# Two 64-row chunks side by side in every transposed tile of a fused attention and FFN kernel

## The chip, the cores and the metric

The kernel runs on one core of a Trainium2 chip. The metric is the device time of one execution in microseconds (us). Shown are the median of three runs and one profiled execution, with the trace of every engine: PE (matrix multiply, its weight loads as PEld), DVE (vector), ACT (scalar), POOL (GpSimd) and SP, which only issues DMAs here. DMAs run on 16 shared DMA engines, from a queue of SP and one of ACT.

## The reference

S = 2048 tokens of D = 448 columns in bf16, 16 heads of 28, a window of 256 tokens, an FFN of 1792.

```python
x = A_x
xn = layernorm(x)                               # mean and variance over the 448 columns
qkv = xn @ wqkv                                 # 448 x 1344, then split into q, k, v of 16 heads of 28
scores = q @ k.T * 28 ** -0.5                   # kept where 0 <= query - key < 256
attn = (softmax(scores) @ v) @ wo
ffn = (gelu(xn @ w_gate) * (xn @ w_up)) @ w_down
out = x + attn + ffn
```

## The kernel before, in words

**Blocks.** The tokens are 16 tiles of 128 (`t`) and four blocks of 512 (`qb`). For every block the kernel makes q, k and v, does windowed attention (`attention`), then gate and up projections with a GELU between (`gated`), and the down projection with the output projection (`gen_down`), which for one block is spread between the attention steps of the next. All instructions stand in an order written out by hand (`tc.manual_schedule()`): the lists `plan` say after which attention step how many steps of a generator are issued, and every engine runs its instructions in the order of the program. A buffer comes free, and a transfer is known to have landed, through semaphores. Each DMA takes the next of eight semaphores, so one is issued only when the DMA eight places earlier has landed.

**The transposed activations.** All projections contract over the 448 columns, which must lie on partitions. 448 is three times 128 and 64 more, or seven chunks of 64 rows, c = 0 to 6. `norm` (L171) or, for tile 1, `norm_scalar` (L180) writes the normalized tile to `xn`; the first four tiles are transposed on PE (`transp`, L192), with a copy out of PSUM into `xnT[:, 0:4, tokens]`, the others by a DMA transpose (`dma_transp`, L188). Before the change, slot m of `xnT` holds rows 128 m to 128 m + 127 for m = 0, 1, 2, that is chunks 2 m and 2 m + 1, and slot 3 holds chunk 6 on both halves of the partitions. For the DMA transposes `norm` writes the last 64 columns twice, with a second instruction; for the first block GpSimd copies the upper half of slot 3 to the lower (L781).

**Two kinds of products.** For the first block, q, k and v take three matmuls over 128 rows (`mm3`, from `v_dense` and `proj`) and one over the 64 rows of chunk 6 (`mm_half`, from `v_half` and `qk_halves`). Two such halves, for q and k or for two token tiles, run at once on the two halves of the array. Everywhere else (`gen_pairs`, `chunk`) two outputs of 64-row products run side by side: the lower half of the partitions takes seven chunks for one output, the upper half seven chunks for another. Each half owns four chunks in `xnT`, and takes the other three from `xsw`, a copy with the halves exchanged that two DMAs make (`swap`, L481). The weights likewise come from their own tiles or from exchanged ones (`wvs` by DMA from memory, `wsq` by `swap_weights`). `own_first` (L331) orders the seven chunks so that a half takes its own four first.

**Weights of q, k and v.** `wv` holds the v columns. `wraw` holds q and k columns as they come; `pads` (L749) copies four heads at a time into `wqp` and `wkp`, with 32 columns a head. Chunk 6 of q (lower half) and of k (upper half) goes to slot 3 of `wraw` and from there, in one DVE copy (L792), to `w3p`. `fill_pads` (L294) later puts the k of the last heads into the spare columns of other heads; for chunk 6 it takes them from `w3k`, which has two DMAs of its own.

**Masks.** In the first four attention steps `masked` (L615) masks probabilities on GpSimd. Later steps multiply by `masks`, 3 x 4 blocks of 64 columns, which `make_masks` (L111) cuts out of ones at the start, one GpSimd select for each half and block that needs one, 18 in all.

**Order of the first stretch.** SP issues, one after the other: x of tile 0, tiles 2 and 3, three slots of `wv`, the first four heads' columns of q and of k, x of tiles 4 to 7, chunk 6 of `wraw` (two) and of `wv` (two), the other columns of q and k, w_up (two), `w3k` (two), the first `swap`. ACT issues x of tile 1 and then loads its function table. PE warms up on zeros, then runs the transposes, the v and the group 0 q and k products, and the scores of step 0 (L688), whose exponentials on ACT (L693) start the attention loop.

Of the kernel before, what the change touches and what calls it, by code (L numbers as in the profile page):

```python
# [17 lines left out]
P = 128  # L18
# [9 lines left out]
def kernel(  # L28
# [55 lines left out]
    wqk = rows(A_wqkv, 0, 3)[:, :, 0:2 * D]  # L84
# [4 lines left out]
    nc.sync.dma_start(out=wv[:, 0:3, :], in_=rows(A_wqkv, 0, 3)[:, :, 2 * D:3 * D])  # L89
    for c in (0, D):  # L90
        nc.sync.dma_start(out=wraw[:, 0:3, c:c + 4 * Dh], in_=wqk[:, :, c:c + 4 * Dh])
    nc.sync.dma_start(out=x_sb[:, 4:8, :], in_=xv[:, 4:8, :])
    for a in range(2):
        nc.sync.dma_start(out=wraw[64 * a:64 * a + 64, 3, 0:D], in_=A_wqkv[384:448, a * D:(a + 1) * D])
# [16 lines left out]
    def make_masks(n):  # L111
        for i, edges in list(enumerate(EDGES))[n]:
            for j, (_, *kinds) in enumerate(edges):
                for h, kind in enumerate(kinds):
                    if kind:
                        m = masks[64 * h:64 * h + 64, i, j, :]
                        nc.gpsimd.affine_select(out=m, in_=m, pattern=[[kind, 64]], compare_op=ALU.is_ge, fill=0.0,
                                                base=min(kind, 0), channel_multiplier=-kind)
# [11 lines left out]
    w3k = const.tile([P, 4 * Dh], bf16, name="w3k")  # L130
    for a in range(2):
        nc.sync.dma_start(out=w3k[64 * a:64 * a + 64, :], in_=A_wqkv[384:448, D + 12 * Dh:2 * D])
# [37 lines left out]

    def norm(t):  # L171
        xn = work.tile([P, 4, P], bf16, name="xn", bufs=4)
        xf = xn[:, :, :].rearrange("p a b -> p (a b)")
        both = ((0, D, 0), (D, 64, 384))
        for lo, n, src in both if t > 3 else both[:1]:
            nc.vector.tensor_scalar(out=xf[:, lo:lo + n], in0=x_sb[:, t, src:src + n], scalar1=mv_all[:, t, 0:1],
                                    scalar2=rstd_all[:, t:t + 1], op0=ALU.subtract, op1=ALU.mult)
        xns[t] = xn
# [315 lines left out]
    def xchunk(qb, hi, c, t0, n):  # L494

        r = slice(64 * hi, 64 * hi + 64)
        if c == 6 or c % 2 == hi:
            return xnT[r, c // 2, t0:t0 + n]
# [582 lines left out]
```

## Time and profile before

| | before |
|---|---|
| median of 3 runs | 211.68 us (211.66 to 211.74) |
| the profiled execution: its time, its span | 211.79 us, 210.1 us |
| PE busy, instructions | 205.1 us (98%), 2837 |
| PEld busy | 98.7 us (47%) |
| DVE busy, instructions | 156.9 us (75%), 360 |
| ACT busy, instructions | 134.5 us (64%), 132 |
| POOL busy, instructions | 44.1 us (21%), 89 |
| DMA moved | 15.68 MB, mean 75 GB/s |
| granted PE clock | 1.00 |

The span runs from the first to the last instruction of the program; the execution's own time is 1.69 us longer. A row of the profile in order of time gives the start in us, the busy us, the engine, the line of the kernel, the operation, what it writes <- what it reads, shapes and a count; in square brackets stands how long the engine had been idle before it, and what ended that. Rows with SPq or ACTq are issues of DMAs: they take that engine's queue, not the transfer. Matmuls overlap in the pipeline and their ends are modelled, so rows overlap. A row of the view by stretches gives start:end, its length, and for PE, PEld, DVE, ACT and POOL the busy us and (count), then the granted clock, the DMA engines' share and GB/s.

### The profile page before, as it was taken

The numbers are of one execution on the slowest core, as the hardware profiler recorded it, in microseconds if no ns is written. First come the engines' busy times: TensorE is split into PE (matmuls) and PEld (weight loads), VectorE is DVE, ScalarE is ACT, GpSimd is POOL, SyncE is SP. The second block draws the span as 40 slices with busy tenths as digits, with TensorE's granted clock in tenths as the row PEclk, the third lists the DMA queues.
The fourth block names the chain that finished last, engine by engine and source line by source line (L and its number), as shares of the span: only waits on it lengthen the run. The fifth ranks groups of instructions, "written<-read, shape, count | busy, mean of one in ns | idle before, by whom it ended". The sixth has DMA issues, their size and how long they took to land. (4 is left out here: it accounts for less than half of the span.)

```text
span 210.1 us, 6672 instructions
## 1 busy us (share of the span) xinstructions
PE 205.1 (98%) x2837; PEld 98.7 (47%) x2842; DVE 156.9 (75%) x360; ACT 134.5 (64%) x132; POOL 44.1 (21%) x89
## 2 busy tenths in 40 slices
PE   7999999999999999999999999999999999999994
PEld 2443454544454545444445544544444454544572
DVE  6898899899788985796438897395385699696532
ACT  4699896866677977423778788523587787756000
POOL 5289922241100220040000102013000022031000
PEclk9999999999999999999999999999999999999999
DMA  6999789984341001003331000100000010100011
GB/s 177 271 235 212 138 187 214 278 269 80 78 100 53 25 22 22 8 5 69 72 75 47 25 3 24 23 3 21 22 5 0 3 47 3 47 7 16 3 47 50
DMA packets 24890, 15.68 MB, mean 75 GB/s; under 512 B 9208, under 2 KB 24728, under 8 KB 24856
## 3 DMA queue, kind: packets, MB, share of 16 engines
q1 hardware_dynamic: 24712, 15.10, 31.5%
q8 instruction: 23, 0.38, 0.7%
q10 hardware_dynamic: 144, 0.11, 0.2%
q14 instruction: 11, 0.09, 0.2%
HBM read 9.26 MB, written 2.41 MB: 56 GB/s over the span
## 5 line engine op out<-in xcount | busy, mean ns | idle before, releaser
L693 ACT ACTIVATE p_sb<-sc 128x2048 bf16<-128x2048 f32 x38 | 71.4, 1879 | 16.9 <-PE sc L688 11.7
L545 ACT ACTIVATE p_sb<-gt 128x1024 bf16<-128x1024 f32 x28 | 28.6, 1025 | 31.1 <-PE gt L505 31.1
L628 POOL TENSOR_TENSOR oN<-oc,l 128x512 bf16<-128x512 f32 x16 | 20.7, 1300 | 120.2 <-DVE l L641 120.2
L505 PE MATMUL gt<-xnT,wg 64*128 64x512 bf16 x224 | 45.6, 376 | 0.0
L414 PE MATMUL po<-wd,hT 128*128 128x448 bf16 (+1 forms) x224 | 44.7, 347 | 0.0
L505 PE MATMUL gt<-xsw,wg 64*128 64x512 bf16 x168 | 40.7, 376 | 0.0
L613 DVE TENSOR_TENSOR p_sb<-p_sb,masks 128x256 bf16<-128x256 bf16 (+1 forms) x98 | 30.8, 368 | 7.4 <-ACT p_sb L693 7.4
L555 DVE TENSOR_TENSOR hT<-p_sb,u 128x512 bf16<-128x512 bf16 x34 | 21.7, 676 | 13.4 <-PE u L505 13.3
L414 PEld LDWEIGHTS <-hT 128*128 128x128 bf16 x238 | 21.9, 98 | 19.1 <-issue 2.2
L505 PEld LDWEIGHTS <-wg 64*128 64x128 bf16 x392 | 19.0, 94 | 22.3
L505 PEld LDWEIGHTS <-wu 64*128 64x128 bf16 x392 | 18.7, 94 | 22.2 <-issue 0.4
L505 PE MATMUL u<-xnT,wu 64*128 64x512 bf16 x136 | 28.1, 376 | 0.0
L505 PE MATMUL u<-xsw,wu 64*128 64x512 bf16 x102 | 24.7, 376 | 0.0
L505 PE MATMUL ue<-xnT,wu 64*128 64x512 bf16 x88 | 18.0, 377 | 0.0
L647 DVE TENSOR_TENSOR oc<-oc,ov 128x512 f32<-128x512 f32 (+1 forms) x16 | 10.5, 656 | 10.0 <-ACT oc L645 9.8
L505 PE MATMUL ue<-xsw,wu 64*128 64x512 bf16 x66 | 16.3, 377 | 0.0
L688 PE MATMUL sc<-qT,kT 28*64 28x320 bf16 (+4 forms) x736 | 16.2, 259 | 0.1
L688 PEld LDWEIGHTS <-kT 28*64 28x64 bf16 x736 | 8.1, 103 | 12.4 <-issue 11.0
L402 DVE TENSOR_TENSOR res<-po,x_sb 128x448 bf16<-128x448 f32 (+1 forms) x14 | 8.1, 605 | 7.9 <-PE po L414 6.7
L522 DVE CAST hT<-ue 128x512 bf16<-128x512 f32 x16 | 10.5, 685 | 2.8 <-PE ue L505 2.8
L645 ACT COPY oc<-ov 128x512 f32<-128x512 f32 x16 | 9.4, 584 | 4.0 <-PE ov L662 4.0
L641 DVE STREAM_TRANSPOSE l<-inv_all 128x512 f32<-128x512 f32 x16 | 11.1, 701 | 0.1
(115 smaller groups left out, 257.3 us busy)
## 6 DMA issues: line engine op xcount, KB each, us to landing
out_dram<-res SPq DMA_DIRECT2D x15, 112.0 KB
wd<-in_B_w_down_dram SPq DMA_DIRECT2D x2, 784.0 KB
x_sb<-in_A_x_dram SPq DMA_DIRECT2D x3, 448.0 KB
xsw<-xnT SPq DMA_DIRECT2D x6, 192.0 KB
wg<-in_B_w_gate_dram SPq DMA_DIRECT2D x2, 560.0 KB
wu<-in_B_w_up_dram SPq DMA_DIRECT2D x4, 224.0 KB
wu<-in_B_w_up_dram SPq DMA_DIRECT2D x2, 336.0 KB
wraw<-in_A_wqkv_dram SPq DMA_DIRECT2D x2, 252.0 KB
```

Of the source, the lines that this page charges most:

```text
L414: nc.tensor.matmul(po[:, 0:w], lhsT=x[:, k, tt * P:(tt + 1) * P], rhs=wt[:, k, lo:up], start=start and n == 0, stop=stop and n == len(term ...
L505: nc.tensor.matmul(ps, lhsT=w[64 * hi:64 * hi + 64, c, p * P:(p + 1) * P], rhs=xchunk(qb, hi, c, qb * QB, QB), start=c == 0, stop=c == 6, ...
L522: copy(out=hTs[qb][:, p + 7 * i, :], in_=us[i])
L545: nc.scalar.activation(out=ges[p][:, :, :], in_=gt[:, :, :], func=ACT.Gelu_apprx_tanh)
L555: nc.vector.tensor_tensor(out=hT[:, p + 7 * i, :], in0=ge[:, i, :], in1=u, op=ALU.mult)
L613: nc.vector.tensor_tensor(out=reg, in0=reg, in1=m, op=ALU.mult)
L628: nc.gpsimd.tensor_tensor(out=oN[:, g, :], in0=oc[:, :], in1=inv, op=ALU.mult)
L641: nc.vector.transpose(out=l1[:, :, :], in_=inv_all[:, 4 * qb + g, :].unsqueeze(2).to_broadcast([P, 16, 32]))
L645: nc.scalar.copy(out=oc[:, :], in_=ov[0][:, :])
L647: nc.vector.tensor_tensor(out=oc[:, q0:], in0=oc[:, q0:], in1=ov[1][:, q0:], op=ALU.add)
L688: nc.tensor.matmul(ss[k0:k0 + nk, j, col:col + nq], lhsT=kT[r, g, kt * P + k0:kt * P + k0 + nk], rhs=qT[r, g, ring(qb).start + q0:ring(qb) ...
L693: nc.scalar.activation(out=p_sb[:, :, 0:ncol], in_=ss[:, :, 0:ncol], func=ACT.Exp, scale=SCALE)
```

## The change

Slot m of `xnT` now holds chunk m on the lower half of the partitions and chunk m + 3 on the upper half, m = 0 to 3, so that the middle chunk, 3, is there twice: in slot 3 below and in slot 0 above. A half therefore owns chunks 0 to 3 or 3 to 6, and takes the other three from `xsw`, whose slot for chunk c is c % 4. The 128-row products take slots 1 to 3 with chunk 0 below as the half (q, and v of even tiles), or slots 0 to 2 with chunk 6 above (k, and v of odd tiles).

- `norm` and `norm_scalar` write all 512 columns of the tile in one instruction, reading x in overlapping runs of 64 (`overlapped`, `halved`). The second instruction of `norm` and the GpSimd copy of 64 rows are gone.
- `wv` and `wraw` are loaded in that order: each DMA (`chunks`, `columns`) fills one half of the partitions, 64 x 4 chunks x some columns. Two of these, half of `wv` and half of the first q columns, are issued by ACT ahead of its table load; the rest by SP. The four DMAs for chunk 6 and the two for `w3k` are gone.
- `w3p` is filled by halves (`pads3`): group 0 on ACT, groups 1 to 3 on GpSimd, in place of the DVE copy. `fill_pads` takes all it needs from `wraw`.
- The masks are cut in six selects over several blocks each, all before the statistics of tile 4.

```diff
+    def chunks(dst, c0, c1, hi, eng=nc.sync):
+        src = A_wqkv[192 * hi:192 * hi + 256, c0:c1].rearrange("(c p) n -> p c n", p=64)
+        eng.dma_start(out=dst[64 * hi:64 * hi + 64], in_=src)
+    def columns(lo, up, hi, k, eng=nc.sync):
+        chunks(wraw[:, :, k * D + lo:k * D + up], k * D + lo, k * D + up, hi, eng)
     nc.scalar.dma_start(out=x_sb[:, 1, :], in_=xv[:, 1, :])
     nc.sync.dma_start(out=x_sb[:, 2:4, :], in_=xv[:, 2:4, :])
-    nc.sync.dma_start(out=wv[:, 0:3, :], in_=rows(A_wqkv, 0, 3)[:, :, 2 * D:3 * D])
-    for c in (0, D):
-        nc.sync.dma_start(out=wraw[:, 0:3, c:c + 4 * Dh], in_=wqk[:, :, c:c + 4 * Dh])
+    chunks(wv, 2 * D, 3 * D, 1, nc.scalar)
+    chunks(wv, 2 * D, 3 * D, 0)
+    columns(0, 4 * Dh, 1, 0, nc.scalar)
+    columns(0, 4 * Dh, 0, 0)
+    for hi in range(2):
+        columns(0, 4 * Dh, hi, 1)
     nc.sync.dma_start(out=x_sb[:, 4:8, :], in_=xv[:, 4:8, :])
-    for a in range(2):
-        nc.sync.dma_start(out=wraw[64 * a:64 * a + 64, 3, 0:D], in_=A_wqkv[384:448, a * D:(a + 1) * D])
-    for a in range(2):
-        nc.sync.dma_start(out=wv[64 * a:64 * a + 64, 3, :], in_=A_wqkv[384:448, 2 * D:3 * D])
-    for c in (0, D):
-        nc.sync.dma_start(out=wraw[:, 0:3, c + 4 * Dh:c + D], in_=wqk[:, :, c + 4 * Dh:c + D])
+    for k in range(2):
+        for hi in range(2):
+            columns(4 * Dh, D, hi, k)
...
     def make_masks(n):
-        for i, edges in list(enumerate(EDGES))[n]:
...
+        flat = masks[:, :, :, :].rearrange("p a b q -> p (a b) q")
+        for h, kind, first, last, step in ((0, 1, 0, 0, 1), (1, 1, 0, 6, 2), (0, 1, 4, 10, 2), (0, -1, 1, 7, 2), (1, -1, 1, 1, 1), (1, -1, 5, 11, 2))[n]:
+            m = flat[64 * h:64 * h + 64, first:last + 1:step, :]
+            nc.gpsimd.affine_select(out=m, in_=m, pattern=[[0, (last - first) // step + 1], [kind, 64]], ...)
...
-    for a in range(2):
-        nc.sync.dma_start(out=w3k[64 * a:64 * a + 64, :], in_=A_wqkv[384:448, D + 12 * Dh:2 * D])
...
+    def overlapped(t):
+        x = x_sb[:, t, :]
+        return bass.AP(x.tensor, x.offset, [list(x.ap[0]), [192, 2], [64, 4], [1, 64]])
+    def halved(xn):
+        return xn[:, :, :].rearrange("p m (i d) -> p i m d", i=2)
     def norm(t):
...
+        nc.vector.tensor_scalar(out=halved(xn), in0=overlapped(t), scalar1=mv_all[:, t, 0:1], scalar2=rstd_all[:, t:t + 1],
+                                op0=ALU.subtract, op1=ALU.mult)
...
-        mm3(pv, lambda c: xnT[:, c, t * P:(t + 1) * P], lambda c: wv[:, c, :], first, not first)
+        m = 1 - t % 2
+        mm3(pv, lambda c: xnT[:, m + c, t * P:(t + 1) * P], lambda c: wv[:, m + c, :], first, not first)
...
+    def pads3(gs, eng=nc.gpsimd.tensor_copy):
+        for hi in range(2):
+            r, hs, c0 = slice(64 * hi, 64 * hi + 64), slice(4 * gs.start, 4 * gs.stop), D * hi
+            src = wraw[r, 3 * hi, c0 + Dh * hs.start:c0 + Dh * hs.stop]
+            eng(out=w3p[r, hs, 0:Dh], in_=src.rearrange("p (h d) -> p h d", d=Dh))
...
-    nc.gpsimd.tensor_copy(out=xnT[0:64, 3, 0:QB], in_=xnT[64:128, 3, 0:QB])
...
-    nc.vector.tensor_copy(out=w3p[:, :, 0:Dh], in_=wraw[:, 3, 0:D].rearrange("p (h d) -> p h d", d=Dh))
+    pads3(slice(0, 1), nc.scalar.copy)
     nc.vector.memset(masks[:, 0, 0, 0:1], 1.0)
-    make_masks(slice(0, 1))
+    make_masks(slice(0, 6))
+    pads3(slice(1, 4))
     stat(4)
     rstd(4, 1)
     stat(5)
     rstd(5, 1)
-    make_masks(slice(1, 3))
...
     def ahead():
-        wv64 = A_wqkv[0:3 * P, 2 * D:3 * D].rearrange("(c h p) n -> h p c n", h=2, p=64)
         for hi in range(2):
-            nc.sync.dma_start(out=wvs[64 * hi:64 * hi + 64, :, :], in_=wv64[1 - hi])
+            w = A_wqkv[256 - 256 * hi:448 - 256 * hi, 2 * D:3 * D].rearrange("(c p) n -> p c n", p=64)
+            nc.sync.dma_start(out=wvs[64 * hi:64 * hi + 64, :, :], in_=w)
```

More of the change, by code (lines that the diff above doesn't have):

```diff
@@ L111, in make_masks @@
     def make_masks(n):
-        for i, edges in list(enumerate(EDGES))[n]:
[L113 to L118, printed above, removed]
+        flat = masks[:, :, :, :].rearrange("p a b q -> p (a b) q")
+        for h, kind, first, last, step in ((0, 1, 0, 0, 1), (1, 1, 0, 6, 2), (0, 1, 4, 10, 2), (0, -1, 1, 7, 2), (1, -1, 1, 1, 1), (1, -1, 5, 11, 2))[n]:
+            m = flat[64 * h:64 * h + 64, first:last + 1:step, :]
+            nc.gpsimd.affine_select(out=m, in_=m, pattern=[[0, (last - first) // step + 1], [kind, 64]], compare_op=ALU.is_ge, fill=0.0,
+                                    base=min(kind, 0), channel_multiplier=-kind)
     minus_half = const.tile([P, 1], f32, name="minus_half")
@@ L266, in q_last @@
         proj(pq, wqp, qb, 3)
[L267 removed]
+        nc.tensor.matmul(pq, lhsT=w3p[:, 12:16, :].rearrange("p h d -> p (h d)"), rhs=xnT[:, 0, qb * QB:(qb + 1) * QB], start=False,
                          stop=True, skip_group_check=True)
```

61 lines of the change are left out of this document (29 added, 32 removed).

## The prediction

> **What bounds the kernel now.** I read the page first, then the busy time of the stretch after the prologue, then the waits of the matmul queue, then the first 15 us in order of time.
>
> ```profile
> PE 205.1 (98%) x2837; PEld 98.7 (47%) x2842; DVE 156.9 (75%) x360; ACT 134.5 (64%) x132; POOL 44.1 (21%) x89
> ```
> ```profile
> 11.90:206.00 194.10, 193.62 (x2774) 93.65 (x2772) 146.77 (x326) 127.56 (x115) 37.92 (x71) 1.00 0.30 66
> ```
> ```profile
> PE wps L152 <- DVE wo L126: 1.4, 1, 1.4
> PE pk L204 <- issue: 0.2, 1, 0.2
> PE pq L204 <- issue: 0.2, 1, 0.2
> ```
>
> From 11.9 us to 206 us PE is busy 193.62 of 194.10 us at full clock, and in the whole run the only matmul that another engine kept waiting over 0.15 us with PE empty is the first. So 0.48 us is about all that any cheaper DVE, ACT, POOL or DMA work can give back behind 11.9 us, and the change leaves the number and the shapes of the matmuls alone. What it does to the time it must do before the first scores at 11.54 us. That stretch, in order of time:
>
> ```profile
> 1.05 0.37 ACTq L87 DMA_DIRECT2D x_sb<-in_A_x_dram  x1
> ...
> 1.27 0.41 SPq L88 DMA_DIRECT2D x_sb<-in_A_x_dram  x1
> ...
> 1.46 1.28 ACT L137 ACT_TABLE_LOAD   x1 [1.46 <-DVE wo L126]
> ...
> 1.73 0.46 SPq L89 DMA_DIRECT2D wv<-in_A_wqkv_dram  x1
> ...
> 3.30 0.49 SPq L92 DMA_DIRECT2D x_sb<-in_A_x_dram  x1
> ...
> 3.75 0.29 ACT L166 ACTIVATE lnv<-mv_all,eps_t 128x1 f32<-128x1 f32 x1 [1.01 <-DVE mv_all L158]
> 3.83 1.21 SPq L94 DMA_DIRECT2D wraw<-in_A_wqkv_dram  x2
> ...
> 4.36 0.36 DVE L176 TENSOR_SCALAR xn<-x_sb,mv_all,rstd_all 128x448 bf16<-128x448 bf16 x1
> ...
> 4.66 0.63 DVE L157 BATCH_NORM_STATS2 st<-x_sb 128x6 f32<-128x448 bf16 x1
> ...
> 5.41 0.76 ACT L184 ACTIVATE xn<-x_sb,nb,rstd_all 128x448 bf16<-128x448 bf16 x1 [0.40 <-POOL nb L183]
> ...
> 6.15 0.39 DVE L200 COPY xnT<-tp 128x512 bf16<-128x512 bf16 x1
> 6.22 0.35 PEld L199 LDWEIGHTS <-xn 128*128 128x128 bf16 x4 [0.51 <-ACT xn L184]
> ...
> 6.63 0.97 PE L204 MATMUL pv<-wv,xnT 128*128 128x448 bf16 x3
> ...
> 8.57 0.33 PEld L204 LDWEIGHTS <-wqp 128*128 128x128 bf16 x3 [0.39 <-DVE xnT L200]
> ...
> 8.68 0.61 POOL L781 COPY xnT<-xnT 64x512 bf16<-64x512 bf16 x1 [3.30 <-DVE xnT L200]
> 8.70 0.73 DVE L792 COPY w3p<-wraw 128x448 bf16<-128x448 bf16 x1 [0.18 <-DMA wraw<-in_A_wqkv_dram]
> ...
> 9.35 0.62 DVE L157 BATCH_NORM_STATS2 st<-x_sb 128x6 f32<-128x448 bf16 x1
> ...
> 9.97 0.39 PE L210 MATMUL s<-xnT,w3p 64*128 64x512 bf16 x2
> ...
> 10.22 0.30 ACT L166 ACTIVATE lnv<-mv_all,eps_t 128x1 f32<-128x1 f32 x1 [1.40 <-DVE mv_all L158]
> ...
> 10.67 0.74 PE L204 MATMUL pv<-wv,xnT 128*128 128x448 bf16 x3
> ...
> 10.83 0.66 DVE L258 CAST kT<-s 128x512 bf16<-128x512 f32 x1
> ...
> 11.54 0.16 PEld L688 LDWEIGHTS <-kT 28*64 28x64 bf16 x16 [0.57 <-DVE kT L258]
> ...
> 13.87 0.39 PE L210 MATMUL pq<-xnT,w3p 64*128 64x512 bf16 x1
> ...
> 14.19 0.43 PE L688 MATMUL sc<-qT,kT 28*64 28x320 bf16 x24
> ```
>
> Two things hold PE here. Up to 6.63 us it waits for xnT of token tiles 0 and 1: statistics and normalization on DVE and ACT, behind the x loads. At 11.54 us the first scores wait for the DVE cast of kT. That cast starts at 10.83, though the last matmul into its bank ended near 10.36 (9.97 + 0.39): DVE was still on stat(5), because the w3p copy took it from 8.70 to 9.43. In between, the w3p matmuls at 9.97 did not wait: w3p was ready at 9.43 and the duplicated 64 rows at 9.29 (8.68 + 0.61), both earlier.
>
> **The change, part by part.**
>
> *What leaves DVE on the path.* The w3p copy (0.73 us) and its 0.18 us wait go. stat(4) could start at 8.52 instead of 9.35, and the cast follows stat(4) by 1.48 us (10.83 - 9.35), so it could start when its bank is full, 10.36 plus a hand-over of some 0.05, and end at 11.07 instead of 11.49. PE cannot use all of that. Its v matmuls start at 10.67 with a pitch near 0.19, so they leave the array at 11.24, and the change from one tile shape to the next costs about 0.1 (13.87 + 0.22 for 512 columns to 14.19). Scores at 11.34: **gain at most 0.20 us** (11.54 - 11.34).
>
> The bound from below is zero, and depends on x tiles 4 to 7, which stat(4) reads. Ahead of their DMA stood 448 KB of x, 336 of wv and 168 of wraw's first heads, 952 in all. With the doubled chunk it is 448 of x, 448 of wv (two halves of 64 x 4 x 448 elements) and 224 of wraw: 1120, so 168 KB (172 thousand bytes) more. The rates come from these two stretches, the first filled by x tiles 4 to 7 into 128 partitions, the second by the w_up loads, which go into 64 partitions at a time:
>
> ```profile
> 6.00:7.00 1.00, 1.00 (x6) 0.54 (x6) 0.88 (x4) 0.94 (x6) 0.00 (x0) 1.00 1.02 341
> ...
> 12.00:13.00 1.00, 0.95 (x5) 0.49 (x6) 1.00 (x4) 1.00 (x2) 0.83 (x4) 1.00 1.14 213
> ```
>
> At 341 to 213 GB/s that is 0.5 to 0.8 us. The old tail chunk of wraw, queued right behind these x tiles, released DVE at 8.70, so they now land at 8.7 at the latest and then between 8.7 and 9.5. A stat(4) at 8.7 gives the cast its full gain, one at 9.35 none. I take 9.1: cast at 10.6, end 11.25, scores near 11.35, so I keep 0.2 but let the range fall to 0.
>
> *What is added on ACT ahead of its first use.* Two more DMA issues (half of wv, a quarter of the first wraw columns) come between the x DMA and the table load. One costs 0.37 on ACT and 0.41 to 0.61 on SP, so the table load starts at 2.2 to 2.7 and ends at 3.5 to 4.0; the first ACTIVATE started at 3.75. **Cost 0 to 0.25**, taken 0.1. Behind it on ACT stand both rstd, the normalization of tile 1 and the copy of its transpose. norm_scalar writes 512 elements for 448: from 0.76 to about 0.85 if it all scaled, and the transposes of tile 1 at 6.22 wait for just that, so +0.06 at least.
>
> *The loads that share the first microseconds.* Half of wv now runs on ACT's queue beside x tiles 2 and 3, which had the engines to themselves. stat(2) started at 4.66, straight after norm(0), so there is no slack. Those x tiles are 229 thousand bytes, 0.67 us at 341 GB/s; if the ACT half takes every second turn from their first byte, they need twice that. **Cost 0 to 0.7**, taken 0.3, since the delay of the table load lies inside it, not on top: both end in a later stat(2), and stat(3), the xnT copy (6.15) and the first v matmul (6.63) move with it. Part comes back: that v matmul spends 0.97 on three matmuls where the later group at 10.67 spends 0.74, so starting later costs up to 0.2 less. Net on PE at 8.57: between -0.1 and +0.5, taken +0.25. wv itself is 112 KB longer; at 213 GB/s that is 0.54 more before the v matmul can start. I have no row that shows when wv lands now, so this is inside the same 0.5.
>
> A rule speaks against this part. The Trainium skill, "SBUF — State Buffer", section "Can I just issue two DMAs to hit both halves?", says that two concurrent DMAs into partitions 0 and 64 gain only 6% over one, and that only a transfer across all 128 partitions reaches all ports. The 213 against 341 GB/s agree in direction. By it every weight half would go at the slow rate, which is the slower case below.
>
> *Off the path.* Masks: 18 selects become two of 64 columns and four of 256, whose nearest rows are these:
>
> ```profile
> L117 POOL TENSOR_SCALAR_AFFINE_SELECT masks<-masks x18: 232/236/318, 9.5 to 15.3; 64x64 bf16<-64x64 bf16 x18
> ```
> ```profile
> L619 POOL TENSOR_SCALAR_AFFINE_SELECT p_sb<-p_sb x24: 407/414/683, 15.6 to 26.5; 64x256 bf16<-64x256 bf16 x24
> ```
>
> From 18 x 0.236 = 4.2 us to 2 x 0.236 + 4 x 0.414 = 2.1 us, and the xnT copy of 0.61 goes too. POOL then starts the first masking of p_sb near 13.9 instead of 15.6, but no matmul waited for it. The two w3p copies for groups 1 to 3, at about 0.46 each (half of 64x512 to all of it, 0.3 to 0.61), must be done by 13.87; POOL has masks until about 10.9, so they hang on the last columns of wraw, below. w3p of group 0 goes to ACT as two small copies of 0.2 to 0.4 each, inside the 1.40 us that ACT sat idle before 10.22; without that cover, L210 at 9.97 would move by the same 0.4 to 0.8.
>
> norm(t) for t above 3 becomes one instruction of 512 elements for two:
>
> ```profile
> L176 DVE TENSOR_SCALAR xn<-x_sb,mv_all,rstd_all 128x448 bf16<-128x448 bf16 x7 | 3.1, 439 | 0.1
> ...
> L176 DVE TENSOR_SCALAR xn<-x_sb,mv_all,rstd_all 128x64 bf16<-128x64 bf16 x4 | 1.6, 405 | 0.0
> ...
> L754 DVE COPY wqp<-wraw 128x336 bf16<-128x336 bf16 x2 | 0.5, 268 | 0.0
> L754 DVE COPY wqp<-wraw 128x672 bf16<-128x672 bf16 x1 | 0.4, 383 | 0.0
> ```
>
> It saves up to 0.4 us twelve times, all under a dense PE: nothing. For tiles 0, 2 and 3 it adds 64 elements; the two wqp copies, also in short runs, cost 0.34 ns an element, so 0.02 each.
>
> The last wraw columns (688 thousand bytes in four halves, behind the x tiles) take 2.0 us at 341 GB/s or 3.2 at 213, so they land between 10.9 and 12.5 where DVE used them at 11.4 to 11.6 and PE needs the k pads at 13.1. Taken at 11.8: DVE waits, PE doesn't. The issue queue has 23 DMAs where 24 stood before the DMA transposes, and the two w3k issues (some 0.6 each) leave from ahead of the swap, whose xsw nobody waited for.
>
> **Sum**, on the profiled execution (211.79 us, span 210.1, 1.69 outside): +0.25 for the start, -0.20 for the cast, 0 for the rest. 210.15 + 1.69 = 211.84; the median of the runs lies 0.11 under that execution, so **211.7 us**: no change that can be told.
>
> **The rivals.**
>
> *Faster.* The halves on two queues fill the engines as well as one wide transfer, x tiles 2 and 3 come no later, and the scores take their 0.20; the wait for xnT at 8.57 (0.39 idle in weight loads, about 0.11 beyond the pitch of 0.19) closes, and a part of the 0.48 in the dense stretch, say 0.15, goes with DVE's lighter load. 211.68 - 0.46 = 211.2. For it: DVE and POOL really are freed. Against it: all three terms must come, and nothing shortens the chain up to 6.63.
>
> *Slower: loads into half the partitions run at the slow rate and decide.* At 213 GB/s the 448 KB of wv take 2.15 us against 1.35 at 341, and the first v matmul, three transposes behind it and the whole matmul queue start 0.8 later; less 0.2 for the slow first matmuls and with no gain at the cast (its x tiles are late too, by 0.8). 211.68 + 0.6 = 212.3. It decides as soon as stat(2) starts after about 5.3 or the first v matmul after about 7.2. By the Trainium skill's rule on two halves this is what happens; the trace bears out the rate, but between rows of w_up, not of wv on two queues.
>
> *It doesn't do what it says: the new norm loses its fast form.* The 512 elements, read in overlapping runs of 64, go at about 1.04 ns each (the 0.63 us of bn_stats over 448 elements is such a row): 0.7 us instead of 0.36 to 0.44. norm(0) then delays stat(2) by 0.3, and norms 2 and 3 the transposes of tile 3 by about 0.5 more, less the slack: 212.2. Against it: the wqp copies in runs of 28 keep 0.34 ns an element.
>
> **How the numbers follow.** Forecast 0.60, faster 0.11, slow halves 0.20, slow norm 0.06, and 0.03 for a last column that lands past 12.5 and holds PE some 0.3 near 13 us. A measurement of this kernel tells about 0.2% (0.42 us) from no change. The forecast's own range is 211.4 to 212.2: the bounds -0.1 - 0.2 and +0.5 - 0 about 211.68. Faster by over 0.2%: 0.11; within: 0.60 and 0.03; slower: the two slow cases, 0.26. The range 211.3 to 212.4 takes in both slow cases and leaves out about 0.15.
>
> **What would show it.** The cast of kT starting at 10.4 to 10.7 and scores at 11.3 to 11.6 show the DVE step right. The start of the table load shows what ACT's two issues cost, stat(2) and the first v matmul (4.66 and 6.63 now) what the shared loads cost; the pads' first use of the last wraw columns shows whether these are late. One norm row near 0.4 us shows that it kept its form. Wrong would be: any PE wait after 12 us that isn't there now, scores before 11.2, or a first v matmul after 7.2.

## The result, and the profile after

The changed kernel takes **212.92 us** (median of 15 runs, 212.07 to 215.61) against 211.74 for the kernel before (15 runs, 211.44 to 212.78). The ratio is 1.0059 with a 95% interval of 1.0042 to 1.0076: it is slower by about 0.6%, outside the range of the prediction and on the side to which it gave 0.26. The longest of the 15 ran at a granted clock of 0.992; without it the longest is 214.23. The profiled execution is one of the shorter ones, 212.24 us with a span of 210.5. Its busy time on the page, and the dense stretch from the first scores on:

```profile
PE 205.4 (98%) x2837; PEld 98.3 (47%) x2842; DVE 153.5 (73%) x347; ACT 135.0 (64%) x134; POOL 42.4 (20%) x78
```
```profile
12.00:206.40 194.40, 193.92 (x2774) 93.51 (x2772) 144.20 (x315) 127.64 (x115) 36.35 (x61) 1.00 0.30 67
```

DVE and POOL were freed as the change promises, by 3.4 and 1.7 us, and PE is as dense as it was: 0.48 us of the stretch is not busy. But the stretch is 0.30 us longer for the same 2774 matmuls (194.40 for 194.10): their records overlap, so a short wait of PE can stand inside its busy time. The loss is a matmul queue that runs later, by one delay ahead of the first scores and one near 35 us. The prologue of the changed kernel in order of time:

```profile
1.48 0.69 ACTq L87 DMA_DIRECT2D wv<-in_A_wqkv_dram  x1
...
2.19 0.63 ACTq L87 DMA_DIRECT2D wraw<-in_A_wqkv_dram  x1
...
2.85 1.28 ACT L140 ACT_TABLE_LOAD   x1 [2.85 <-DVE masks L139]
...
4.15 0.29 ACT L169 ACTIVATE lnv<-mv_all,eps_t 128x1 f32<-128x1 f32 x1
...
4.71 0.41 DVE L185 TENSOR_SCALAR xn<-x_sb,mv_all,rstd_all 128x512 bf16<-128x512 bf16 x1 [0.29 <-ACT rstd_all L170]
...
5.04 0.62 DVE L160 BATCH_NORM_STATS2 st<-x_sb 128x6 f32<-128x448 bf16 x1
...
5.50 0.81 ACT L193 ACTIVATE xn<-x_sb,nb,rstd_all 128x512 bf16<-128x512 bf16 x1 [0.40 <-POOL nb L192]
...
6.97 0.74 PE L212 MATMUL pv<-wv,xnT 128*128 128x448 bf16 x3
...
8.67 0.33 PEld L212 LDWEIGHTS <-wqp 128*128 128x128 bf16 x3 [0.39 <-DVE masks L813]
...
8.71 2.18 POOL L123 TENSOR_SCALAR_AFFINE_SELECT masks<-masks 64x64 bf16<-64x64 bf16 x6 [3.25 <-DVE masks L813]
8.82 0.59 ACT L775 COPY w3p<-wraw 64x112 bf16<-64x112 bf16 x2
...
9.42 0.63 DVE L160 BATCH_NORM_STATS2 st<-x_sb 128x6 f32<-128x448 bf16 x1 [0.79 <-DMA x_sb<-in_A_x_dram]
...
10.90 0.66 DVE L268 CAST kT<-s 128x512 bf16<-128x512 f32 x1
...
11.62 0.16 PEld L701 LDWEIGHTS <-kT 28*64 28x64 bf16 x16 [0.54 <-DVE kT L268]
...
12.42 0.55 DVE L768 COPY wkp<-wraw 128x336 bf16<-128x336 bf16 x1 [0.67 <-DMA wraw<-in_A_wqkv_dram]
...
13.20 0.81 PE L212 MATMUL pk<-xnT,wkp 128*128 128x512 bf16 x3
```

The first v matmul is 0.34 us late (6.97 for 6.63), wins 0.23 of it back (three matmuls in 0.74 for 0.97), and PE is 0.10 late at 8.67. DVE then stands idle for 0.79 us, waiting for x tiles 4 to 7, so the cast of kT starts at 10.90 although the w3p copy is gone, and the scores come at 11.62 for 11.55. From there the two kernels run 0.08 us apart up to 32 us. There GpSimd scales `oN` (L628 before, L641 after). In order of time, before:

```profile
31.88 1.27 POOL L628 TENSOR_TENSOR oN<-oc,l 128x512 bf16<-128x512 f32 x1 [4.13 <-DVE l L641]
```
```profile
32.90 0.41 DVE L613 TENSOR_TENSOR p_sb<-p_sb,masks 128x256 bf16<-128x256 bf16 x1
```
```profile
34.92 0.37 PE L353 MATMUL pk<-xnT,wkp 64*128 64x512 bf16 x1
```

and after:

```profile
32.32 1.27 POOL L641 TENSOR_TENSOR oN<-oc,l 128x512 bf16<-128x512 f32 x1 [5.62 <-DVE v_sb L250]
```
```profile
32.97 0.77 DVE L626 TENSOR_TENSOR p_sb<-p_sb,masks 128x256 bf16<-128x256 bf16 x1
```
```profile
35.32 0.37 PE L362 MATMUL pk<-xnT,w3p 64*128 64x512 bf16 x1
```

The product on GpSimd starts 0.44 us later, 0.36 more than the rest of the kernel. Its row names a cast of `v_sb` on DVE as what released it, but the product does not read `v_sb`. In the trace GpSimd's wait for `l` ends at 31.86 (31.78 before), so the product starts 0.46 us after that wait where it was 0.10. The row names that cast because it ended 0.01 us ahead of the product. The mask multiply on DVE takes 0.77 for 0.41 us, the casts of qT and kT behind it follow late, and the matmul that waits for kT's bank comes 0.40 late (35.32 for 34.92). This 0.32 on top of the 0.08 stays to the end: 0.40 in the matmuls and 0.05 behind the last one make the 0.45 us between the two spans. The median of the runs lost 1.18, so the median run loses 0.7 more than the profiled one.

### The profile page after: what moved, and what is told of

Read it like the earlier page. It is cut to its first block, busy times and chain, and to the rows that moved or that the text cites. A ratio compares the mean times of both kernels' runs of the same rounds, so it can differ in the third digit from the quotient of the medians.

```text
span 210.5 us, 6650 instructions
## 1 busy us (share of the span) xinstructions
PE 205.4 (98%) x2837; PEld 98.3 (47%) x2842; DVE 153.5 (73%) x347; ACT 135.0 (64%) x134; POOL 42.4 (20%) x78
## 3 DMA queue, kind: packets, MB, share of 16 engines
HBM read 9.35 MB, written 2.41 MB: 56 GB/s over the span
## 5 line engine op out<-in xcount | busy, mean ns | idle before, releaser
L641 POOL TENSOR_TENSOR oN<-oc,l 128x512 bf16<-128x512 f32 x16 | 20.7, 1300 | 122.5 <-DVE l L654 116.9
L518 PE MATMUL gt<-xsw,wg 64*128 64x512 bf16 x168 | 43.9, 376 | 0.0
L518 PE MATMUL u<-xsw,wu 64*128 64x512 bf16 x102 | 27.1, 376 | 0.0
L518 PE MATMUL ue<-xsw,wu 64*128 64x512 bf16 x66 | 17.4, 377 | 0.0
```

Source lines behind the costliest of these rows:

```text
L518: nc.tensor.matmul(ps, lhsT=w[64 * hi:64 * hi + 64, c, p * P:(p + 1) * P], rhs=xchunk(qb, hi, c, qb * QB, QB), start=c == 0, stop=c == 6, ...
L641: nc.gpsimd.tensor_tensor(out=oN[:, g, :], in0=oc[:, :], in1=inv, op=ALU.mult)
```

## The experiments

In some places below, the time at which a load landed is given. It is the time of the last update of the load's semaphore in the trace.

Three theories stood at the start. A: loads land late by an amount that varies from run to run, the last columns of wraw above all. B: GpSimd and DVE hold each other up near 32 us, by chance or always. C: ACT's two DMA issues delay its table load and with it the start.

**The changed kernel twice more.** No edit; the question is where a median run loses.

> The changed kernel once more, for a second trace. The profiled execution of the changed kernel was among its fastest (212.24 where the runs spread from 212.07 to 215.61). Theory A (the last wraw columns land late, by an amount that differs from run to run): the DVE copy of the k columns that waited until 12.33 us is released at another time, and an execution over 213 us shows PE waiting between 12.5 and 15 us. Theory B (GpSimd's scaling of the output and DVE's mask multiplies block each other near 32 us): the stretch up to 30 us is the same within 0.1 us, and what differs is the PE wait near 35 us, 0 to 0.4 us, and others of its kind later.

> As the run before: a third trace of the changed kernel. A: the spread between executions lies in waits for DMAs before 20 us. B: it lies in waits behind GpSimd and DVE after 30 us.

Measured: 212.48 and 212.86 us. In the second, in order of time:

```profile
10.04 0.63 DVE L160 BATCH_NORM_STATS2 st<-x_sb 128x6 f32<-128x448 bf16 x1 [1.42 <-DMA x_sb<-in_A_x_dram]
...
12.24 0.42 PE L701 MATMUL sc<-qT,kT 28*64 28x320 bf16 x16 [0.73 <-DVE kT L268]
```

The wait of DVE for x tiles 4 to 7 is now 1.42 us, and the scores are 0.70 late. The step at 35 us is the same 0.32 to 0.33 in all three profiles: it is no chance collision. The x tiles land at 9.39, 9.65 and 10.02, though their DMA is issued at 4.49 in all three. Later profiles of kernels with the same loads fit the same sum:

| kernel | statistics of tile 4 start (us) | scores against before | last matmul against before |
|---|---|---|---|
| changed | 9.42 | +0.08 | +0.40 |
| changed, again | 9.67 | +0.33 | +0.65 |
| changed, again | 10.04 | +0.70 | +1.02 |
| all loads on SP | 10.16 | +0.82 | +1.14 |
| w3k kept | 10.22 | +0.88 | +1.20 |
| one GpSimd memset more | 10.33 | +0.98 | +0.97 |

Except in the last row, where the step at 35 us is missing, the last matmul is the scores' delay plus 0.32. That sum leaves nothing for the columns of wraw, which were the first suspicion.

**Both DMA issues of ACT moved to SP.**

```diff
-    chunks(wv, 2 * D, 3 * D, 1, nc.scalar)
+    chunks(wv, 2 * D, 3 * D, 1)
-    columns(0, 4 * Dh, 1, 0, nc.scalar)
+    columns(0, 4 * Dh, 1, 0)
```

> The two weight loads that ACT issues ahead of its table load are issued by SP, in the same place of the order. Theory C (they cost the start 0.34 us, since the first ACTIVATE came at 4.15 instead of 3.75): the first ACTIVATE is back at 3.75, the statistics of tile 2 start when x lands, near 4.7, and the first v matmul at 6.65 to 6.8; but SP issues everything behind them 1.3 us later, so x tiles 4 to 7 and the last wraw columns land later still: stat(4) near 9.6 to 10.2, scores at 11.8 to 12.4. By A the median is then 213 to 214.5 and the spread is no smaller. By C alone the median falls to 212.5 or less.

Measured: 212.88 us (4 runs), 1.0049 (1.0032 to 1.0066). ACT has its table as early as before, and nothing is won. In order of time:

```profile
1.73 1.48 SPq L87 DMA_DIRECT2D wv<-in_A_wqkv_dram  x2
...
3.25 2.59 SPq L87 DMA_DIRECT2D wraw<-in_A_wqkv_dram  x4
...
5.89 0.60 SPq L103 DMA_DIRECT2D x_sb<-in_A_x_dram  x1
```

The DMA of x tiles 4 to 7 is issued at 5.89 instead of 4.49 (3.30 in the kernel before), and the tiles land at 10.14. An issue 1.40 us later made them land only 0.1 to 0.75 later than in the three profiles above. The first v matmul comes at 7.14 and not at 6.65 to 6.8 as expected; the second half of wv lands at 7.01, just ahead of it. The delay of ACT is real, and small beside the x tiles.

**The six selects alone, on the kernel before.** Only `make_masks` and its calls as in the change.

> The kernel before with the six mask selects alone. POOL starts the first masking of p_sb near 13.9 instead of 15.6. My account: 211.7, no change within 0.2%, since no matmul waited for it. B, if it is the earlier GpSimd work that brings the collision near 32 us: up to 0.4 us slower, with a DVE mask multiply of 256 columns over 0.6 us long just before the qT and kT casts at 33 to 35 us.

Measured: 211.72 us (10 runs), 0.9999 (0.9990 to 1.0009). The masks cost and bring nothing.

**The late GpSimd product: place in its stream or in memory.**

```diff
     nc.gpsimd.memset(v_sb[:, :, :, Dh + 1:32], 0.0)
+    nc.gpsimd.memset(v_sb[:, 0, :, Dh:Dh + 1], 1.0)
```

> The changed kernel with one more small GpSimd memset (column 28 of v_sb of tile 0, written again) near 2 us, so that every later GpSimd instruction stands one place further in its stream. In all four profiles of the changed kernel the GpSimd product at 32 us starts 0.46 us after the last of its waits, in the kernel before and with the six selects alone 0.09 to 0.10 after it. Theory 'place in the stream' (the late start belongs to the position of that instruction among GpSimd's): it starts 0.09 to 0.10 after its wait and the step of 0.33 us near 35 us is gone. Theory 'place in memory': nothing changes, 0.46 and 0.33 stay.

```diff
+    w3k = const.tile([P, 4 * Dh], bf16, name="w3k")
+    nc.vector.memset(w3k[:, 0:1], 0.0)
```

> The changed kernel with the 224 bytes of w3k kept as a buffer (one DVE memset of one column, nobody reads it), so that what is allotted behind it lies where it lay in the kernel before. Theory 'place in memory': the GpSimd product at 32 us starts 0.09 to 0.10 after its wait and the step of 0.33 us near 35 us is gone. Theory 'place in the stream': 0.46 and 0.33 stay.

Measured: 212.91 and 213.05 us, both with late x tiles. The rows of the two, memset first:

```profile
32.87 1.27 POOL L642 TENSOR_TENSOR oN<-oc,l 128x512 bf16<-128x512 f32 x1 [5.29 <-DVE l L655]
```
```profile
33.12 1.27 POOL L643 TENSOR_TENSOR oN<-oc,l 128x512 bf16<-128x512 f32 x1 [5.66 <-DVE v_sb L252]
```

With the memset it starts 0.10 us after its wait ended and the step at 35 us is gone; with the buffer it starts 0.46 after it, as in every profile of the changed loads without a memset. The place in GpSimd's stream decides, not the place in memory.

Why that place is slow is not shown. One thing in the traces goes with it without exception. The trace lists DMA queues of the kind "instruction"; one of them, q14, moves blocks of 8 KB. After a block near 20 us the next one starts at 21.8 to 25.5 us in the twelve profiles where the product starts 0.10 after its wait, and at 33.3 to 40.6, always behind the product, in the eight where it starts 0.46 after. So the product may be the first instruction of a new block there; no run was made to test that. In the eight the product also starts within 0.01 us of the end of the `v_sb` cast, which always ends 0.52 behind `l`; that it waits for the cast to leave some shared path is a rival that no run excludes, though in the kernel before the two run side by side.

**The two statistics moved away from before the cast.** First far behind, into and past step 0, in both kernels:

```diff
-    stat(4)
-    rstd(4, 1)
-    stat(5)
-    rstd(5, 1)
...
         stat(7)
+        rstd(4, 1)
+        rstd(5, 1)
         rstd(6, 2)
...
-            plan = [[last_v, lambda: stat(6), (u, 3), ahead], ...
+            plan = [[last_v, lambda: stat(6), (u, 3), lambda: stat(4), lambda: stat(5), ahead], ...
```

> The changed kernel with the statistics of tiles 4 and 5 issued after the first k and q products of step 0 instead of ahead of the kT cast. In four profiles of the changed kernel and its variants the first of these statistics waited for x tiles 4 to 7 until 9.39, 9.65, 10.02 and 10.14 us, and the first scores came at 11.62, 11.87, 12.25 and 12.36. Theory 'landing': this wait on DVE is all of the run-varying loss, so the cast starts at 10.4 to 10.6 in every run, scores near 11.4, 0.2 less spread than before, and the median falls by 0.4 to 0.7, to 212.2 to 212.5 from some 212.9, with the 0.33 us near 35 us left. Rival 'columns': the last k columns of wraw land at 12.0 to 13.0 and the DVE copies behind them hold the matmuls of group 1 as well; then part of the gain is given back between 13 and 16 us, the median stays at 212.6 or more and the spread over 0.5.

> The same move of the two statistics on the kernel before, nothing else. The cast of kT there waits for DVE, not for a matmul: it starts at 10.83 with its bank full near 10.4. Theory 'landing' has the cast at 10.4 to 10.5 and scores at 11.34, as the prediction's DVE step worked it out: 211.55 against 211.75. If something else holds the scores (the v matmuls from 10.67 on), or the statistics are in the way later, no change: 211.75.

Measured: 215.68 and 216.81 us. Both expectations missed, because the move put GpSimd's scale of tile 5 behind the masking of p_sb. In the kernel before with this move, in order of time:

```profile
11.28 0.42 PE L688 MATMUL sc<-qT,kT 28*64 28x320 bf16 x16
...
19.65 0.57 POOL L164 TENSOR_TENSOR rstd_all<-lnv,minus_half 128x1 f32<-128x1 f32 x1
...
20.25 0.77 DVE L176 TENSOR_SCALAR xn<-x_sb,mv_all,rstd_all 128x448 bf16<-128x448 bf16 x2 [2.56 <-POOL rstd_all L164]
20.93 0.68 DVE L258 CAST kT<-pk 128x512 bf16<-128x512 f32 x1
```

The scores do come 0.27 early at 11.28, and then DVE waits 2.56 us for that scale with the next cast of kT behind it. By 23 us this kernel is 4.97 us behind, and it stays so to the last matmul; what cost the part beyond that wait is open.

Then directly behind the cast:

```diff
-    stat(4)
-    rstd(4, 1)
-    stat(5)
-    rstd(5, 1)
...
     qk_copies(0, 0, pq, pk)
+    stat(4)
+    stat(5)
+    rstd(5, 1)
     pads(nc.vector.tensor_copy, wqp, slice(1, 2))
     v_copy(0, pvs[0], nc.scalar.copy)
     v_copy(1, pvs[1], nc.scalar.copy)
+    rstd(4, 1)
```

> The changed kernel with the kT cast issued ahead of the statistics of tiles 4 and 5 on DVE (the scale of tile 5 on GpSimd behind them, that of tile 4 on ACT behind the first two v copies); DVE does the same work in all. The earlier move past step 0 had the cast at 10.4 but put GpSimd's scale of tile 5 behind the masking of three steps, so that DVE waited 2.6 us for it; here it stays ahead of them. Theory 'landing': cast at 10.4 to 10.6, scores near 11.5 in place of 11.6 to 12.5, the step of 0.33 near 35 us stays: 212.1 to 212.3. Rival 'columns': the copies into wkp wait for the last k columns (landed 12.1 to 13.0 so far) and hold the matmul that was at 13.13 by 0.2 to 0.5 (0.47 in the earlier move): then 212.4 to 212.8 and a spread over 0.4.

> The same order on the kernel before, nothing else. In the earlier move the cast there started early enough for scores at 11.28 against 11.55, and the matmuls stayed 0.27 early until 18.05. Theory: this gain of 0.2 to 0.27 now reaches the end, 211.5. Rival: the statistics behind the cast make the copies into wqp and wkp late and hold the matmul at 13.13, or the normalizations at 15.7 move and hold 18.26: 211.7 or more.

Measured: 212.89 us (4 runs), 1.0053 (1.0036 to 1.0070), and 212.35 (8 runs), 1.0028 (1.0017 to 1.0039). Missed again. The kernel before in this order:

```profile
10.42 0.69 DVE L258 CAST kT<-s 128x512 bf16<-128x512 f32 x1 [1.00 <-PE s L210]
...
12.50 0.31 DVE L754 COPY wqp<-wraw 128x336 bf16<-128x336 bf16 x1
```
```profile
12.87 0.82 PE L204 MATMUL pq<-xnT,wqp 128*128 128x512 bf16 x2 [0.44 <-DVE wqp L754]
```

The cast comes first and the copy into wqp last, and the next matmul, at 12.48 in the kernel before, waits for that copy. That is 0.39 of the 0.65 us by which its last matmul is late; the other 0.26 is lost between 18 and 23 us. In the changed kernel the cast starts at 10.71 and the scores at 11.62, and the same matmul waits until 13.11. In both moves the gain at the cast was lost again at what DVE then did later: it had no slack to trade in this stretch.

**Halves or bytes.** On the kernel before, the three loads cut into halves of the partitions (same bytes), or 168 KB added to all partitions:

```diff
-    nc.sync.dma_start(out=wv[:, 0:3, :], in_=rows(A_wqkv, 0, 3)[:, :, 2 * D:3 * D])
+    halves = (slice(64, 128), slice(0, 64))
+    for r in halves:
+        nc.sync.dma_start(out=wv[r, 0:3, :], in_=rows(A_wqkv, 0, 3)[r, :, 2 * D:3 * D])
     for c in (0, D):
-        nc.sync.dma_start(out=wraw[:, 0:3, c:c + 4 * Dh], in_=wqk[:, :, c:c + 4 * Dh])
+        for r in halves:
+            nc.sync.dma_start(out=wraw[r, 0:3, c:c + 4 * Dh], in_=wqk[r, :, c:c + 4 * Dh])
```

> The kernel before with wv and the first q and k columns loaded by halves of the partitions, the same bytes in the same layout: three DMAs become six, all from SP. Theory 'rate' (a load into 64 partitions goes slower, and each has an issue of its own): the x tiles 4 to 7 and the chunk behind them, which DVE waited for until 8.7 to 8.9, land 0.5 to 1.0 later, the cast and the scores with them, 212.2 to 212.7, and the runs spread. Theory 'bytes' (only the 168 KB that the doubled chunk adds count): no change, 211.75.

```diff
+    nc.sync.dma_start(out=x_sb[:, 12:14, 0:336], in_=A_wqkv[0:P, 0:672].rearrange("p (t n) -> p t n", t=2))
     nc.sync.dma_start(out=x_sb[:, 4:8, :], in_=xv[:, 4:8, :])
```

> The kernel before with one more DMA of 168 KB to all 128 partitions ahead of x tiles 4 to 7, into a part of x_sb that is loaded later again (nobody reads it): the bytes that the doubled chunk adds ahead of these tiles, without the halves. Theory 'bytes': they land 0.5 to 0.8 later (172 thousand bytes at 341 to 213 GB/s), DVE's copy to w3p starts at 9.2 to 9.5 in place of 8.7 to 8.9, and the cast and the scores come as much later: 212.2 to 212.5. Theory 'rate': less than half of what the halves alone cost, 211.75 to 212.0.

Measured: 214.16 us (4 runs, 213.11 to 215.20), 1.0102 (1.0052 to 1.0152), and 212.48 (6 runs), 1.0036 (1.0024 to 1.0049). DVE's wait for the DMA behind the x tiles and the scores, with halves:

```profile
10.17 0.28 DVE L795 COPY w3p<-wraw 128x448 bf16<-128x448 bf16 x1 [1.76 <-DMA wraw<-in_A_wqkv_dram]
```
```profile
12.57 0.42 PE L691 MATMUL sc<-qT,kT 28*64 28x320 bf16 x16 [0.62 <-DVE kT L261]
```

with the bytes:

```profile
9.56 0.28 DVE L793 COPY w3p<-wraw 128x448 bf16<-128x448 bf16 x1 [1.13 <-DMA wraw<-in_A_wqkv_dram]
```
```profile
11.96 0.42 PE L689 MATMUL sc<-qT,kT 28*64 28x320 bf16 x16 [0.62 <-DVE kT L259]
```

Against 8.70 in the kernel before, DVE starts 0.86 us later for the bytes and 1.47 for the halves. (The copy itself then takes 0.28 in place of 0.73, with no GpSimd copy beside it, so the scores lose 0.41 and 1.02.) The x tiles, which lie ahead of that chunk, land at 8.28 in the kernel before, at 9.07 with the bytes and at 9.64 with the halves: 0.79 and 1.36 later. Both theories hold, and the halves weigh more. The two runs do not part bytes and issues cleanly, since the added load also moves the issue of the x tiles from 3.30 to 3.83. What shows in the run with halves is the queue: each half has an issue of its own, the DMA of x tiles 4 to 7 is issued at 5.79 for 3.30, and the engines run dry meanwhile. Stretches of the run with halves, in the columns described above:

```profile
6.00:7.00 1.00, 0.77 (x8) 0.44 (x7) 0.86 (x4) 0.94 (x6) 0.00 (x0) 1.00 0.39 68
7.00:8.00 1.00, 1.00 (x12) 0.68 (x11) 0.65 (x4) 0.91 (x3) 0.00 (x0) 1.00 0.68 134
```

The DMA engines are busy 0.39 and 0.68 of these two microseconds, at 68 and 134 GB/s against 341 and 218 in the kernel before. In the changed kernel, where ACT issues two of the halves, they do not run dry. Its stretches behind 8 us:

```profile
8.00:9.00 1.00, 1.00 (x8) 0.40 (x6) 0.43 (x2) 1.00 (x3) 0.24 (x2) 1.00 1.15 234
9.00:10.00 1.00, 1.00 (x6) 0.29 (x3) 0.58 (x1) 0.38 (x2) 0.95 (x3) 1.00 1.18 225
```

The engines are busier than before (shares 1.15 and 1.18 for 0.93 and 1.00) and move less (234 and 225 GB/s for 287 and 269). So there a lower rate shows, and not engines that run dry between issues; whether the half partitions, the shorter rows or the second queue lower it, no run separates. The profile of the halves is of one of the two longer runs (215.08 and 215.20; the others took 213.11 and 213.24). It lost a further 1.9 us behind the scores, most of it near 33.7 us, where the v matmuls wait for an exchanged xsw.

**Fewer bytes ahead of the cast.** In the changed kernel x tiles 6 and 7 go behind the other columns of q and k; then with the GpSimd memset; then with the unread chunks left out of the loads as well (chunk 3 on the upper half of q, and on the lower half of the first k columns, 70 KB):

```diff
-    nc.sync.dma_start(out=x_sb[:, 4:8, :], in_=xv[:, 4:8, :])
+    nc.sync.dma_start(out=x_sb[:, 4:6, :], in_=xv[:, 4:6, :])
     for k in range(2):
         for hi in range(2):
             columns(4 * Dh, D, hi, k)
+    nc.sync.dma_start(out=x_sb[:, 6:8, :], in_=xv[:, 6:8, :])
```

> The changed kernel with x tiles 4 and 5 loaded where tiles 4 to 7 were, and tiles 6 and 7 behind the other columns of q and k. DVE's statistics ahead of the kT cast read only tiles 4 and 5. Theory 'landing': 224 KB fewer lie ahead of them, 0.67 to 1.08 us at 341 to 213 GB/s, so they land at 8.6 to 9.5 in place of 9.4 to 10.3; the columns come that much earlier too (11.4 to 12.3). Scores at 11.3 to 11.7, the step of 0.33 near 35 us stays: 212.0 to 212.4, spread below 0.5. Rival 'queue': the time is lost in the issues of half-partition DMAs, not in bytes; then one issue more ahead of nothing that is saved gives 212.7 or more.

> The same with the one small GpSimd memset more that made the GpSimd product at 32 us start 0.10 after its wait. Theory 'place in the stream': 0.33 less than the kernel with the split alone, 211.7 to 212.1. If the step of 0.33 was not on the path to the end: the same as with the split alone.

> Split and memset, and the chunks that nobody reads left out of the loads: chunk 3 on the upper half of the q columns, and on the lower half of the first k columns, 70 KB in all, 28 of them ahead of x tiles 4 and 5. Theory 'landing': another 0.1 us at these tiles and 0.2 to 0.3 at the last columns: at most 0.1 under the one without the cut, 211.6 to 212.0, against 211.75 for the kernel before.

Measured: 212.04 us (10 runs, 211.97 to 212.18), 1.0015 (1.0006 to 1.0024); 211.85 (10 runs, 211.66 to 213.08), 1.0021 (1.0005 to 1.0037); 211.86 (12 runs, 211.67 to 213.69), 1.0022 (1.0004 to 1.0039). The split alone, in order of time:

```profile
8.54 0.62 DVE L161 BATCH_NORM_STATS2 st<-x_sb 128x6 f32<-128x448 bf16 x1
...
10.53 0.69 DVE L269 CAST kT<-s 128x512 bf16<-128x512 f32 x1 [0.43 <-PE s L219]
```
```profile
11.44 0.42 PE L702 MATMUL sc<-qT,kT 28*64 28x320 bf16 x16
```

DVE no longer waits for x, the cast waits for its own matmul, and the scores come 0.10 before those of the kernel before. 0.88 us of the loss and nearly all of the spread are gone: 'landing' holds. The rival 'queue', by which the issues and not the bytes cost the time, expected 212.7 or more and is out: the DMA of tiles 4 and 5 is issued at 4.49 as before and, with half the bytes, lands at 8.41. The step at 35 us stays, as expected. With the memset it goes: the shortest runs of the last two are 211.66 and 211.67, and in the profile of the last one the final matmul is 0.11 before that of the kernel before. But 3 of 10 and 3 of 12 of their runs take 212.7 to 213.7, so the medians improve by less than 0.2. The profile with the memset alone (211.94) shows one such loss: between 58 and 62 us its matmuls fall back 0.19 us, where a weight load waits 0.4 us for `oN` on GpSimd, which waits for a DMA. Whether the longer runs lose there, no trace shows.

**One place further.** Two memsets in place of one.

> The changed kernel with split x tiles, without the unread chunks, and with two small GpSimd memsets more in place of one. Theory 'place in the stream': only the one position is slow, so the GpSimd product starts 0.10 after its wait again and most runs take 211.65 to 211.75; if the longer runs (4 of 12 with one memset were at 212 or more) belong to that one shift they are gone, if they belong to the memsets as such they stay.

Measured: 211.78 us (12 runs, 211.68 to 213.52), 1.0019 (1.0002 to 1.0036). The product starts 0.10 after its wait again, so of the places tried only one is slow. The longer runs stay (four over 212.2). None of them was profiled, and the kernel of the next experiment, with no memset, has such runs too; where they lose is open.

**The same split on the kernel before, and one DMA more.**

```diff
-        nc.sync.dma_start(out=x_sb[:, 12:16, :], in_=xv[:, 12:16, :])
+        for t in (12, 14):
+            nc.sync.dma_start(out=x_sb[:, t:t + 2, :], in_=xv[:, t:t + 2, :])
```

> The kernel before with x tiles 6 and 7 moved behind the other columns of q and k in the same way. DVE waited there 0.18 us for the chunk behind the x tiles; that wait goes (224 KB fewer ahead of it), the cast and the scores come up to 0.18 earlier: 211.6 to 211.75.

> The kernel before with the load of x tiles 12 to 15 (near 32 us, nobody waits for it) cut into two DMAs; the bytes are the same. Each DMA takes the next of eight semaphores, and at the end SP waits for all eight in a fixed order, some 0.06 us each. Theory 'order of the semaphores': the last store comes to stand on the first of them instead of the last, the other seven are looked at after it landed: last matmul unchanged, 0.4 to 0.45 us more at the end, 212.15. Rival: the half load or its issue holds something, then the last matmul moves as well; or nothing: 211.7.

Measured: 212.07 us (11 runs), 1.0017 (1.0009 to 1.0026), and 212.12 (8 runs), 1.0029 (1.0013 to 1.0044). The split was to gain up to 0.18 and lost 0.37 with its last matmul 0.02 us early. The second kernel shows why. Its last two stores, in order of time, and those of the kernel before, each under the heading line of the answer:

```profile
core 0 of [0], span 210.4 us
...
207.05 0.84 SPq L407 DMA_DIRECT2D out_dram<-res  x2
```
```profile
core 0 of [0], span 210.1 us
...
207.12 0.84 SPq L407 DMA_DIRECT2D out_dram<-res  x2
```

The stores are issued 0.07 us earlier, and the execution is 0.37 longer (212.16 against 211.79). In the trace SP's last eight waits, one for each DMA semaphore, stand in a fixed order some 0.06 us apart. In the kernel before seven of them pass before the last store lands at 209.18, and the eighth ends at 209.22. With one DMA more that store falls on the first semaphore: it lands at 209.11, the seven others follow, and the eighth ends at 209.59. The 0.73 us of the 168 KB load is in part this: its scores are 0.41 late, the rest is at the end. The changed kernel itself pays only 0.05 there.

None of these kernels is faster than the kernel before by more than the runs scatter.

## Why the prediction was wrong, step by step

- **DVE step: failed, and it is the main cause.** The prediction put the landing of x tiles 4 to 7 between 8.7 and 9.5, took 9.1, and called the worst case a gain of zero. They landed at 9.4 to 10.3 in six profiles. Past 9.35 every delay goes straight into the scores, so the term had no floor at zero: the scores came 0.08 to 0.98 late where 0.20 gained was entered. What the term left out is the halves. It priced the loads by their bytes, and for bytes it was right: with the 168 KB alone the tiles land at 9.07, 0.79 later, inside its 0.5 to 0.8. That loads into halves of the partitions also delay what lies behind them had no term in the forecast: not the later issue of the x tiles, though it had up to 0.61 us for an issue on SP, and not the slow rate, which it left to the slower rival (x tiles late by 0.8). The halves alone cost 1.36 with no byte added. In that run the issues on SP show as the reason; in the changed kernel the engines stay busy and move 225 to 234 GB/s, and why the tiles land at 9.39 in one execution and 10.02 in another is open. That the cast would start when its bank is full, with the scores gaining up to 0.20, was right as soon as the tiles were there: 10.53 and 11.44 with the split.
- **"Off the path": wrong at one place.** The text expected no PE wait after 12 us that isn't there before. There is one at 35 us, 0.32 in every profile of the change itself, from a GpSimd product that starts late. The masks, the copies and the pads on GpSimd are as cheap as computed (six selects until 10.9, the w3p copies 0.46 and 0.47), but they left that product at a slow place in the stream. No row of before could show this.
- **ACT's two issues: right in kind, too small.** Table load at 2.85, not 2.2 to 2.7, since a half load takes ACT 0.63 to 0.69 us to issue where 0.37 to 0.61 was taken; first ACTIVATE 0.39 later instead of 0 to 0.25.
- **Shared loads: no delay of x tiles 2 and 3.** stat(2) at 5.04 follows norm(0) (4.71 to 5.12 overlapping) without a wait for a DMA; they land at 4.67 where it was 4.64. Net on PE before the k and q products: +0.10 measured, +0.25 taken, inside the bounds; the slow first matmuls gave back 0.23 where up to 0.2 was named. That the net came out inside is in part luck: the prediction took 0.3 from loads that delay x, and what was paid was the table load on ACT.
- **Last wraw columns:** 12.33 us where 11.8 was taken and 10.9 to 12.5 was the range (in later runs up to 13.0). "DVE waits, PE doesn't" held: DVE idles 0.67, and the k product is at 13.20 for 13.13, the same 0.08 as the scores.
- **norm of 512 elements:** 0.41 us; the rival of a slow norm is out. (Its 1.04 ns an element is not what the row it names gives: 0.63 us for 448 elements is 1.41. Either way its price is 0.7 us.) The masks alone measured as no change, as predicted.
- **The slower rival had the cause and not the place.** It let loads into halves decide through wv and the first v matmul, past 7.2, for 212.3. The v matmul came at 6.97; what decided were the x tiles queued behind the halves, with the step at 35 us on top, 212.92. Its 0.20 should have been more: the Trainium skill, "SBUF — State Buffer", section "Can I just issue two DMAs to hit both halves?", that two transfers into the two halves hardly gain on one, speaks for it, and the run with halves alone agrees in direction (x tiles 1.36 us later); there the visible reason is the issue time.

## What to carry to other kernels

Price a load that is cut in two by the issues that it adds to its queue and by the rate that its halves reach, and not by its bytes alone. Look for the DMA behind it whose landing an in-order engine waits for ahead of the work that matters: a row that waits 0.18 us today has no floor when more is queued before it. A change in the number of DMAs or of one engine's instructions can move the time by 0.3 to 0.4 us by itself; compare the last matmul and the rows of other places before the edit is blamed.

## What the runs showed of the hardware that was not expected

- A GpSimd product starts 0.46 us after its last wait at one place in its stream and 0.10 at three others (with one and two memsets more, and in the kernel before). In all twenty profiles the late start goes with a block on an instruction queue that is moved behind the product and not ahead of it; that this is the reason is not shown.
- GpSimd holds up a DVE instruction with two inputs in SBUF. The mask multiply took 0.77 us and ended at 33.74, 0.15 after the product on GpSimd (32.32 + 1.27); before, it took 0.41 and ended at 33.31, again about 0.15 after it. The Trainium skill, "SBUF — State Buffer", section "Who interferes with whom", says that such an instruction contends with a GpSimd instruction that reads SBUF, and the rows agree.
- The landing of the same loads varies by 0.6 us between three executions of one program (9.42, 9.67, 10.04), while ten runs of the split kernel, whose DVE does not wait for them, lie within 0.2 us. What makes it vary is open.
- The end of this program costs 0.4 us more or less by which of eight semaphores its last store falls on, and so by the number of its DMAs (span 210.4 against 210.1 us, with earlier stores).
